# Windowed attention and a gated feed-forward on one core: another opening order, group 0's gate by Gelu, and four more blocks' x transposed by TensorE

## The chip, the core and the metric

The kernel runs on one core of a Trainium2 chip. The time is that of the device in microseconds for one execution, median of several. A profile of one execution gives each engine's instructions; the engines are TensorE (PE for matmuls, PEld for weight loads), VectorE (DVE), ScalarE (ACT), GpSimd (POOL) and SyncE (SP, which here only issues DMAs).

## The reference

Attention with 4 sink keys and a window of 128 keys, then a feed-forward layer with the quick Gelu. Inputs are float32; q, k and v are 4 x 8 x 768 x 64.

```python
scores = scale * np.matmul(q, k.transpose(0, 1, 3, 2))      # scale = 1/8
keep = is_sink | in_window                                    # key < 4, or 0 <= query - key < 128
scores = np.where(keep, scores, -1000000000.0)
a = np.exp(scores - np.max(scores, axis=-1, keepdims=True))
a = a / (np.sum(a, axis=-1, keepdims=True) + 1e-09)
x = np.matmul(a, v)        # heads side by side: 3072 x 512
h = x @ w_in               # 512 x 2048
g = h * (1.0 / (1.0 + np.exp(-1.702 * h)))
return g @ w_out           # 2048 x 512
```

## The kernel before

The 3072 rows are 24 blocks of 128 queries (6 for each of the 4 batch entries) and 12 groups of two blocks. All matmuls are in float16.

**Loads.** POOL issues, with a cast on the way, q, k and v of each block and the two weights in four pieces each (`w_in`, `w_out`). Block 0's q and k are loaded raw by SP (`rawq`, `rawk`) and cast by ACT or DVE. SP also issues the constants (`ident`, the mask `bias0`, `later`, and others), the DMA transposes and the outputs.

**Attention of a block.** q and k are transposed: for blocks 0 to 7 by PE (`tq`, L442, then a copy by ACT or DVE into `qkT`), for the rest by a DMA transpose. PE makes the scores of the 8 heads against the block's own keys (`own`, two tiles of 4 heads) and against those of the block before (`prv`), and against the sinks (`snk`). For block 0 PE first writes the mask into `own` (L489). DVE merges `own` and `prv` into one tile, since each query needs one of the two for each column (L565), takes the maximum (`mx`, L577), joins that of the sinks, and subtracts it (`e`, L632); ACT takes exp (`a`, L664). For blocks 0 to 3 one of the two halves is not subtracted by DVE: ACT takes exp from `own` with the maximum as bias, head by head (L618, bias `nb`). The result is transposed (`at`): by PE for blocks 0 to 3 (`ta`, L727), by DMA from SP for the rest (L761). POOL splits `at` into the columns of the own and of the previous block by two selects (L676 into `atp`, L670 in place). PE multiplies by v (`av`, L782 for the sinks, L788, L792), with a column of ones that gives the sum; DVE divides (L803, L804) into `xn`. `xn` is transposed into `xT`: by PE for blocks 0 to 3 (`tx`, L817, and a copy), by one DMA transpose for each group of two blocks after that (L830).

**Feed-forward of a group.** Eight units of `hT` (L852, into tiles of a ring named mm), each followed by its gate into `gT`: by ACT's Gelu (L882), or, in group 0, by ACT's tanh (L866) and a DVE step (L873), since tanh lies in the table that exp uses and Gelu in another (ACT_TABLE_LOAD). Then 16 matmuls for each block of the group (`o`, L903), a copy to `osb` and a store.

**Order.** Every step is an `Op` with an engine (or a choice of two), a cost, dependencies and buffers. `Plan.run` is a list scheduler: at each time it takes for each engine the ready step with the lowest key, and the order that it finds is written out as fixed instruction lists for all engines. The keys are a long list of numbers in the file, `KEYS`. Nothing is rescheduled on the chip: an engine, or a DMA queue, that waits for one step holds all that stand behind it.

Of the kernel before, what the change touches and what calls it, by code (L numbers as in the profile page):

```python
# [11 lines left out]
FP32 = mybir.dt.float32  # L12
# [7 lines left out]
P = 128  # L20
D = 64
# [9 lines left out]
    tx=(0, 1, 2, 3),  # L31
# [4 lines left out]
    tanh=(0,),  # L36
# [6 lines left out]
    sel2=(),  # L43
    steady=8,
# [10 lines left out]
512 736 367 602 310 550 170 2 181 458 338 312 41 456 211 67 413 484 39 69 10 35 90 100 306 46 134 13 203 194 247 206  # L55
29 390 176 216 256 251 370 426 301 489 604 578 150 778 128 562 881 72 614 513 42 504 253 755 644 539 48 533 276 782
679 567 55 559 296 805 710 594 61 587 320 827 740 624 68 617 345 844 766 658 78 648 379 857 793 690 92 681 407 867
813 720 107 712 436 878 152 236 882 900 27 94 466 541 425 476 862 561 460 553 112 798 137 350 264 400 218 221 668
488 153 811 230 771 608 315 470 175 32 47 508 330 186 243 26 743 24 858 44 171 49 396 257 119 51 823 195 872 77 611
60 87 641 172 145 224 897 63 120 600 629 767 54 835 191 104 369 303 378 291 233 547 166 14 22 56 138 187 234 792 328  # L60
419 454 592 657 57 713 28 189 523 86 122 260 212 638 8 480 429 366 299 467 725 279 4 322 106 437 406 635 787 358 814
34 125 747 342 742 158 165 239 374 207 548 748 609 53 178 442 705 870 149 45 443 527 38 329 397 140 483 110 242 441
244 463 190 709 240 353 776 777 200 884 516 12 507 91 139 84 105 6 219 544 473 352 490 435 210 403 74 141 272 281 3
534 869 582 98 143 123 156 384 274 494 293 30 215 445 115 468 135 797 155 368 616 59 924 840 292 646 228 915 324 5
919 524 469 847 214 676 151 677 245 62 398 269 96 749 275 249 496 530 580 519 918 667 517 238 621 491 340 325 505
317 669 88 250 300 331 627 923 551 495 860 227 706 167 707 259 71 430 288 108 773 294 262 520 556 606 545 922 698
543 255 653 514 372 348 535 343 699 102 268 326 355 660 926 354 252 448 220 738 184 280 83 311 121 318 283 546 584
639 571 925 730 570 278 687 540 399 383 560 376 731 113 287 349 388 692 928 607 542 880 263 763 197 764 302 97 486
337 142 820 344 305 574 613 672 599 927 754 598 298 716 568 431 410 588 404 756 133 309 385 417 722 930 640 569 888
284 790 213 791 327 109 509 365 159 838 377 332 603 643 701 632 929 781 631 323 745 595 461 438 618 433 783 154 336  # L70
411 447 750 932 446 319 526 270 812 226 351 126 395 177 405 356 634 678 733 665 931 804 664 347 770 625 487 471 649
464 806 168 362 439 478 774 934 702 630 896 333 832 248 833 386 144 564 427 188 864 434 389 666 708 760 695 933 826
694 381 795 659 510 497 682 493 828 185 394 472 499 800 936 734 663 901 357 850 261 851 414 162 590 459 204 875 465
418 697 739 786 727 935 843 724 408 817 691 537 521 714 515 845 198 424 498 525 821 282 387 566 905 450 492 273 82
908 877 193 314 911 295 1 440 20 209 633 36 619 671 626 572 402 522 148 573 265 101 552 174 662 452 118 232 428 799
75 809 229 834 11 339 235 50 477 93 304 726 500 161 721 647 444 9 173 475 579 593 160 765 80 116 899 815 759 183 892
127 202 65 132 179 231 290 920 363 474 601 409 258 655 518 382 768 703 313 596 674 199 412 686 31 16 40 853 124 70
217 673 0 117 364 416 201 359 785 23 371 577 375 81 415 719 916 79 19 95 7 784 266 622 485 735 675 696 66 52 391 549
531 129 131 819 222 420 511 873 729 267 903 451 822 597 15 271 650 807 285 654 506 761 704 728 76 58 421 576 557 146
147 837 237 449 538 883 753 286 906 481 839 628 17 289 683 829 307 688 536 788 737 752 89 64 453 605 585 163 164 852  # L80
254 479 565 889 780 308 910 502 854 661 18 316 715 846 334 717 563 808 762 779 103 73 482 637 615 180 182 863 277
501 591 893 803 335 912 529 865 693 21 341 744 859 360 746 589 830 789 802 114 85 503 670 645 192 196 874 297 528
623 898 825 361 913 555 876 723 25 373 769 868 392 772 620 848 810 824 136 99 532 700 680 205 208 885 321 554 656
902 842 393 914 583 886 751 33 401 794 879 422 796 651 861 831 841 157 111 558 732 711 223 225 890 346 581 689 904
856 423 917 612 891 775 37 432 816 887 455 818 685 871 849 855 169 130 586 757 741 241 246 894 380 610 718 907 866
457 921 642 895 801 43 462 836 909 684 758 652 636 575
# [154 lines left out]
def kernel(  # L241
# [32 lines left out]
    plan = Plan(RING)  # L274

# [22 lines left out]

    def hw(key, cost, fn, xfer, **kw):
        return plan.add(SP, key, cost, fn, xfer=xfer, post=1.3, **kw)  # L300

    o_ident = hw(-99, 0.4, lambda: nc.sync.dma_start(ident, ident_d.ap()), 0.1)
    o_bias0 = hw(-98, 0.4, lambda: nc.sync.dma_start(bias0, bias0_d.ap()), 0.1)
    o_later = hw(-97, 0.4, lambda: nc.sync.dma_start(later, later_d.ap()), 0.1)
    o_bias1 = hw(-96, 0.4, lambda: nc.sync.dma_start(bias1, bias1_d.ap()), 0.1)
    o_kept = hw(-94.5, 0.4, lambda: nc.sync.dma_start(kept, kept_d.ap()), 0.1)
    o_own = hw(-95, 0.4, lambda: nc.sync.dma_start(ownm, own_d.ap()), 0.1)
# [14 lines left out]
    def sw(key, cost, fn, xfer, **kw):  # L322
        return plan.add(POOL, key, cost, fn, xfer=xfer, post=2.6, **kw)
# [12 lines left out]

    def load_block(which, b, key, after=0.0):
        bb, r = divmod(b, 6)
        i = b % 2
        src = {"q": q, "k": k, "v": v}[which][bb, :, r * P : (r + 1) * P, :].rearrange("h s d -> s h d")  # L340
        if which == "v":
            return sw(key, 0.88, lambda: nc.gpsimd.dma_start(v65[:, b, :, 0:D], src), 1.0, deps=[z_1], after=after)  # L342
        w = "qk".index(which)
        buf = qkn[b // 2]
        if b in CFG["f32"]:
            raw = const.tile([P, H, D], FP32, name=f"raw{which}{b}")
            o_raw = hw(-120 + w, 0.4, lambda: nc.sync.dma_start(raw, src), 0.9)
            return plan.add(
                {DVE: 0.45, ACT: 0.6}, -95 + w, 0, lambda e: copy(e, buf()[:, i, w], raw), deps=[o_raw], take=[buf]
            )  # L350
        return sw(
            key, 0.88, lambda: nc.gpsimd.dma_start(buf()[:, i, w], src), 0.9,  # L352
            take=[buf], after=after,
        )
# [70 lines left out]
    o_qkt, o_ks, o_own_s, o_x = {}, {}, {}, {}  # L425

    for b in range(NBLK):
# [8 lines left out]
        if b in CFG["tq"]:  # L436
# [8 lines left out]
            for w in range(2):  # L445
                a = plan.add(
                    PE, K0 - 48 + w, 0.45 if b < 2 else 0.35, lambda w=w, f=t_qk: f(w), deps=[ld["qk"[w] + str(b)], o_ident],
# [37 lines left out]
        snk = ps("mi", (P, 4, 2, 4), FP32, f"snk{b}")  # L485
# [18 lines left out]
        if b in CFG["pemask"]:  # L504
            s_msk = plan.add(
                PE, K0 - 41, 0.9 if b == 0 else 0.43, lambda own=own, f=masks: f(own), deps=[o_bias0, o_identb] + (o_qkt[b] if b else []), take=own,
                slack=slack["s"],
            )
        s_own = None if both else plan.add(
            PE, K0 - 40, 0.5 if b < 2 else 0.24, lambda b=b, own=own, f=scores: f(own, b),  # L510
# [26 lines left out]
        if r > 0:  # L537

            def sinks(b=b, bb=bb, snk=snk):
                for j in range(4):  # L540
                    nc.tensor.matmul(snk()[:, j], qk_of(b)[:, j], ksb[:, bb, j], start=True, stop=True)

            s_snk = plan.add(PE, K0 - 40, 0.15, sinks, deps=([s_own] if b >= CFG['steady'] else []) + o_qkt[b] + [o_ks[bb]], take=[snk], give=[qkt[g]], slack=slack["s"])
# [69 lines left out]
        for l in range(2):  # L613
            if l >= 2 - nb:

                def exps(l=l, own=own, a16=a16, nbias=nbias):
                    for j in range(4):
# [7 lines left out]
                        ACT, K0 - 36.5, 1.02, exps, deps=[o_nb, z_a[b % RING["a16"]]],  # L625
# [18 lines left out]
        if r > 0:  # L644
# [9 lines left out]
            subs.append(plan.add(DVE, K0 - 38.7, 0.15, sub_s, deps=[top], take=[e32], give=[snk]))  # L654
# [99 lines left out]
        else:  # L754
            o_exp = plan.add(
                ACT, K0 - 36, 1.02, lambda a16=a16, e32=e32, w=w, f=exp: f(a16, e32, 0, w),
                deps=subs + zero, take=[a16], give=[e32], table="exp", slack=slack["e"],
            )
# [3 lines left out]
                deps=[o_exp], take=[at], give=[a16], xfer=1.35, post=0.8,  # L762
# [49 lines left out]
        if b in CFG["tx"]:  # L812
# [6 lines left out]
            o_tx = plan.add(PE, K0 - 28, 0.35, t_x, deps=norms, take=[tpx], give=[xn])  # L819
# [108 lines left out]
    order = plan.run()  # L928
    with tc.manual_schedule():
        for op in order:  # L930
            op.emit(op.on) if len(op.eng) > 1 else op.emit()
# [35 lines left out]
```

## Time and profile before

| what | value |
|---|---|
| median of 3 runs | 240.04 us (239.17 to 246.06) |
| the profiled execution | 240.28 us, its span 238.6 us |
| PE busy | 216.5 us (91%) |
| DVE busy | 141.2 us (59%) |
| ACT busy | 133.8 us (56%) |
| POOL busy | 114.2 us (48%) |
| mean granted TensorE clock | 0.985 |
| table loads on ACT | 20 of 1.28 us |

The span is cut into 40 slices of about 6 us; a digit is the busy share of an engine in one slice in tenths. The windows list for each stretch the stretch, its length, then busy time with the number of instructions for PE, PEld, DVE, ACT and POOL, the granted clock, the busy time of the DMA engines and the rate in GB/s. The chain gives start, length, and what the end of the program is traced back to.

### The profile page before, as it was taken

What the parts mean: (1) busy time and instruction counts of PE and PEld (TensorE: products, weight loads), DVE (VectorE), ACT (ScalarE), POOL (GpSimd) and SP (SyncE); (2) the same over time, 40 slices, a digit from 0 to 9 for tenths busy, and PEclk for the clock granted to TensorE, in tenths of its full rate; (3) what the DMA queues carried; (4) which work ended last, traced back from release to release, by engine and by line L of the source; (5) the groups of instructions that cost most, each with busy time, mean ns of one, the idle gap of its engine ahead of it and who ended that gap; (6) DMA issues with size and microseconds to landing.
All of it is one profiled execution on the core that took longest, in us unless ns stands there. A gap on an engine that the chain in (4) does not pass through costs nothing.

```text
span 238.6 us, 5359 instructions
## 1 busy us (share of the span) xinstructions
PE 216.5 (91%) x2173; PEld 152.6 (64%) x2173; DVE 141.2 (59%) x344; ACT 133.8 (56%) x203; POOL 114.2 (48%) x130
## 2 busy tenths in 40 slices
PE   0368899899977999999999999999999999999994
PEld 0237598777436758648659568578577685685763
DVE  4279989827934556788598639767676571120000
ACT  3256686577226665737837565565666648351521
POOL 8878689199505618619708449644051210700000
PEclk9999769999999999999999999999999999999999
DMA  8999999999999997999999999999992223530202
GB/s 115 182 161 192 199 200 179 138 127 115 133 157 256 149 152 140 149 195 161 140 171 171 163 204 178 143 180 173 124 206 47 49 64 69 145 91 0 88 3 88
DMA packets 134152, 33.38 MB, mean 140 GB/s; under 512 B 126672, under 2 KB 131184, under 8 KB 134128
## 3 DMA queue, kind: packets, MB, share of 16 engines
q0 software_dynamic: 77024, 13.37, 73.8%
q1 hardware_dynamic: 57104, 19.67, 46.0%
q8 instruction: 17, 0.28, 0.5%
q14 instruction: 7, 0.06, 0.1%
HBM read 27.49 MB, written 6.29 MB: 142 GB/s over the span
## 4 chain that ended last, share of the span: by engine, by line
PE 76%; DMA 10%; DVE 7%; ACT 3%; SPq 1%; issue 1%; ACTq 0%; DVEq 0%
PE hT L852 33%; PE o L903 29%; DMA xT<-xn 7%; DMA bias<-cbias 3%; PE av L788 2%; PE av L792 2%; PE av L782 2%; PE own L522 2%; DVE mx L577 2%; DVE own L565 1%; DVE gT L873 1%; PE prv L522 1%; DVE xn L804 1%; DVE e L632 1%; PE ta L727 1%; PE tq L442 1%
## 5 line engine op out<-in xcount | busy, mean ns | idle before, releaser
L852 PE MATMUL hT<-xT,w_in 128*128 128x256 f16 (+1 forms) x832 | 93.5, 265 | 2.6 <-DMA xT<-xn 2.2
L903 PE MATMUL o<-w_out,gT 128*128 128x512 f16 (+1 forms) x400 | 90.2, 371 | 0.0
L852 PEld LDWEIGHTS <-w_in 128*128 128x128 f16 x832 | 74.6, 98 | 15.9 <-DMA xT<-xn 3.2
L882 ACT ACTIVATE gT<-hT 128x512 f16<-128x512 f32 x88 | 51.8, 597 | 41.7 <-PE hT L852 41.6
L676 POOL TENSOR_SCALAR_AFFINE_SELECT atp<-at 128x1024 f16<-128x1024 f16 (+1 forms) x23 | 22.5, 979 | 89.0 <-DMA at<-a 76.8
L903 PEld LDWEIGHTS <-gT 128*128 128x128 f16 x400 | 36.9, 98 | 35.0
L565 DVE COPY_PREDICATED own<-later,prv 128x512 f32<-128x512 uint16 x40 | 26.0, 691 | 18.0 <-PE prv L522 17.2
L577 DVE TENSOR_REDUCE mx<-own 128x4 f32<-128x512 f32 x48 | 31.1, 683 | 2.0 <-PE own L497 1.9
L664 ACT ACTIVATE a<-e 128x1056 f16<-128x1056 f32 (+3 forms) x27 | 24.5, 918 | 13.8 <-DVE e L632 6.8
L632 DVE TENSOR_TENSOR e<-own,mx 128x512 f32<-128x512 f32 x44 | 28.7, 682 | 0.5
L329 DVE COPY osb<-o 128x512 f32<-128x512 f32 (+1 forms) x7 | 4.6, 654 | 32.6 <-PE o L903 30.3
L333 ACT COPY osb<-o 128x512 f32<-128x512 f32 (+1 forms) x16 | 9.1, 572 | 25.8 <-PE o L903 25.8
L670 POOL TENSOR_SCALAR_AFFINE_SELECT at<-at 128x1024 f16<-128x1024 f16 (+1 forms) x23 | 22.4, 972 | 1.6
L342 POOL DMA_DIRECT2D v<-in_v_dram x24 | 21.7, 913 | 0.0
L352 POOL DMA_DIRECT2D qkn<-in_q_dram x23 | 21.0, 911 | 1.1 <-POOLq L948 0.8
L804 DVE TENSOR_TENSOR xn<-av,rcp 128x256 f16<-128x256 f32 x48 | 20.4, 425 | 1.7
L352 POOL DMA_DIRECT2D qkn<-in_k_dram x23 | 20.6, 898 | 0.3 <-DMA qkn<-in_q_dram 0.2
L803 DVE RECIPROCAL rcp<-av 128x4 f32<-128x4 f32 x48 | 8.4, 176 | 18.0 <-PE av L792 17.2
L788 PE MATMUL av<-v,at 128*128 128x65 f16 x192 | 17.5, 198 | 0.1
L788 PEld LDWEIGHTS <-at 128*128 128x128 f16 x192 | 14.9, 100 | 1.3
L442 PE MATMUL tq<-ident,qkn 128*128 128x128 f16 x64 | 7.6, 282 | 8.8 <-DMA ident<-cident 8.8
L792 PE MATMUL av<-v,atp 128*128 128x65 f16 x160 | 15.4, 197 | 0.0
(57 smaller groups left out, 180.7 us busy)
## 6 DMA issues: line engine op xcount, KB each, us to landing
out_dram<-osb SPq DMA_DIRECT2D x23, 256.0 KB, 2.6
v<-in_v_dram POOLq DMA_DIRECT2D x24, 128.0 KB, 6.2
qkn<-in_q_dram POOLq DMA_DIRECT2D x23, 128.0 KB, 6.3
qkn<-in_k_dram POOLq DMA_DIRECT2D x23, 128.0 KB, 5.7
w_in<-in_moe_w_in_dram POOLq DMA_DIRECT2D x4, 512.0 KB, 8.6
w_out<-in_moe_w_out_dram POOLq DMA_DIRECT2D x4, 512.0 KB, 11.2
at<-a SPq DMA_TRANSPOSE x20, 3.5
rawk<-in_k_dram SPq DMA_DIRECT2D x1, 256.0 KB
```

The costliest lines, as they stand in the source:

```text
L352: key, 0.88, lambda: nc.gpsimd.dma_start(buf()[:, i, w], src), 0.9,
L565: nc.vector.copy_predicated(out=own[l](), mask=later.unsqueeze(1).to_broadcast((P, 4, P)), data=prv[l]())
L577: lambda l=l, own=own, small=small: nc.vector.tensor_reduce(out=small[:, l], in_=own[l](), axis=AX.X, op=ALU.max),
L632: nc.vector.tensor_tensor(out=e32()[:, 512 * l : 512 * l + 512].rearrange("p (j s) -> p j s", j=4), in0=own[l](), in1=small[:, l].unsqueez ...
L664: nc.scalar.activation(out=a16()[:, lo:hi], in_=e32()[:, lo:hi], func=AF.Exp, scale=scale)
L670: nc.gpsimd.affine_select(out=dst()[:, lo : lo + n], in_=at()[:, lo : lo + n], pattern=[[0, n], [1, P]], compare_op=ALU.is_ge, fill=0.0, b ...
L676: nc.gpsimd.affine_select(out=dst()[:, lo : lo + n], in_=at()[:, lo : lo + n], pattern=[[0, n], [-1, P]], compare_op=ALU.is_gt, fill=0.0, ...
L788: nc.tensor.matmul(av()[:, j], ato()[:, c], v65[:, b, h], start=(r == 0), stop=(r == 0))
L804: nc.vector.tensor_tensor(out=xn()[:, i].rearrange("p (j l) d -> p l j d", l=2)[:, l], in0=av()[:, :, 0:D], in1=rcp.unsqueeze(2).to_broadc ...
L852: nc.tensor.matmul(ht()[:, n], w_in16[:, c, bass.ts(f, P)], xt[g]()[:, tok, c], start=(c == 0), stop=(c == 3))
L882: lambda fs=fs, cols=cols, gt=gt, ht=ht: nc.scalar.activation(out=gt()[:, fs[0] : fs[-1] + 1, cols], in_=ht(), func=AF.Gelu_apprx_sigmoid),
L903: nc.tensor.matmul(po(), gt()[:, F, bass.ts(t, P)], w_out16[:, F, cols], start=(F == 0), stop=(F == NF - 1))
```

## The change

- Four blocks more (4 to 7) have x transposed by PE and copied, where groups 2 and 3 used the DMA transpose.
- Group 0's gate is ACT's Gelu; the DVE step and the tanh are gone.
- Raw q of block 0 is SP's first DMA, raw k the first on ACT's queue; `ident` and `bias0` follow on SP, and the table `kept` is not loaded.
- PE gets matmuls on a zeroed tile (`fill`) into columns 256 to 511 of a bank whose first 32 columns hold the sinks' scores. Their number ahead of each step comes from the gaps of PE in the plan between 1.5 and 45; there are 38, of which 15 are PE's first instructions.
- Some costs that the plan works with are changed, and `KEYS` is another list, so the order of all engines' work is another. In the first blocks, PE takes a unit of `hT` of group 0 before block 2's scores, and POOL issues the four pieces of `w_out` after block 1's selects.
- The division of the first blocks' shift between DVE and ACT (`nb`) is as before. `chain` is set so that it does nothing, and the cuts of exp in the last part of the diff are one piece wherever they are used.

```diff
 CFG = dict(
-    tx=(0, 1, 2, 3),
+    tx=(0, 1, 2, 3, 4, 5, 6, 7),
...
-    tanh=(0,),
+    tanh=(),
...
+    fill=(1.5, 45.0, 0.15, 0.11),
+    chain=99,
+    gap=3,
...
 KEYS = [ (another list of the same length and kind)
...
+    misc = psp.tile([P, 512], FP32, tag="mi", bufs=1, name="misc")
...
-    o_ident = hw(-99, 0.4, lambda: nc.sync.dma_start(ident, ident_d.ap()), 0.1)
...
+    raw, o_raw = {}, {}
+    for b in CFG["f32"]:
+        for w, e in (("q", nc.sync), ("k", nc.scalar)):
...
+            o_raw[w, b] = hw(-3000, 0.4, lambda dst=raw[w, b], src=src, e=e: e.dma_start(dst, src), 0.7)
+    o_ident = hw(-2000, 0.4, lambda: nc.sync.dma_start(ident, ident_d.ap()), 0.1)
+    o_bias0 = hw(-1999, 0.4, lambda: nc.sync.dma_start(bias0, bias0_d.ap()), 0.1)
...
+    fill = const.tile([P, 2 * P], FP16, name="fill")
+    z_f = plan.add(DVE, -2000, 0.1, lambda: nc.vector.memset(fill, 0.0))
...
-        snk = ps("mi", (P, 4, 2, 4), FP32, f"snk{b}")
+        snk = Buf("mi", lambda: misc[:, 0:32].rearrange("p (j l s) -> p j l s", l=2, s=4))
...
     order = plan.run()
+    idle, last = {}, 1.0
+    if CFG["fill"]:
+        lo, hi, rest, one = CFG["fill"]
+        for op in order:
+            if op.on == PE:
+                a, z = max(last, lo), min(op.start, hi)
+                for b in o_snk:
+                    if o_snk[b].start < z and o_sub[b].done + 0.5 > a:
+                        a = max(a, min(z, o_sub[b].done + 0.5))
+                idle[op] = max(0, int((z - a - rest) / (one if a > 6.0 else 2 * one)))
+                last = op.end
     with tc.manual_schedule():
         for op in order:
+            for n in range(idle.get(op, 0)):
+                nc.tensor.matmul(misc[:, 256:512], fill[:, 0:P], fill, start=True, stop=True)
             op.emit(op.on) if len(op.eng) > 1 else op.emit()
```

## The prediction, made before the changed kernel was run

> **What bounds the kernel now.** First the page's busy shares and the 40 slices (6 us each), to see which engine is full when.
>
> ```profile
> PE 216.5 (91%) x2173; PEld 152.6 (64%) x2173; DVE 141.2 (59%) x344; ACT 133.8 (56%) x203; POOL 114.2 (48%) x130
> ...
> PE   0368899899977999999999999999999999999994
> ...
> DVE  4279989827934556788598639767676571120000
> ...
> PEclk9999769999999999999999999999999999999999
> ```
>
> PE is full from slice 8 to the last one, except in slices 11 and 12; before slice 8 it is not, and there DVE is. So two stretches can give time: the start, and 66 to 75 us. From 90 us on PE has no idle time that the windows show, so nothing is won there unless PE has less to do. The profiled execution took 240.28 us with a span of 238.6; the median of the runs is 240.04, so I work from 240.28 and treat the two as equal.
>
> Next the chain of waits over the start, which says what opens it:
>
> ```profile
> 4.51 6.83 DMA bias<-cbias
> 11.38 1.01 PE own L489 x2
> 12.39 0.43 PE tq L442 x4
> 12.82 0.56 PE own L497 x8
> 13.40 1.30 DVE mx L577 x2
> ```
>
> The first maximum runs at 13.40 because the mask table, the last of eight transfers at the head of SP's queue, lands at 11.38. From there to 46.85 (the end of block 5's second subtraction) DVE is busy without a real gap: windows of 3 us show 2.66 to 2.97 from 15 to 45. That is the bound of the first stretch.
>
> Then the second stretch, as windows (PE busy first) and as the chain:
>
> ```profile
> 66.00:69.00 3.00, 2.50 (x12) 0.94 (x10) 0.90 (x2) 1.54 (x2) 0.00 (x0) 1.00 2.56 143
> 69.00:72.00 3.00, 1.59 (x20) 0.76 (x20) 1.49 (x3) 0.53 (x1) 0.00 (x0) 1.00 2.01 159
> 72.00:75.00 3.00, 1.75 (x16) 1.58 (x17) 0.99 (x2) 1.94 (x3) 0.83 (x1) 1.00 0.72 231
> ...
> 87.00:90.00 3.00, 2.64 (x32) 1.87 (x32) 0.14 (x1) 2.92 (x4) 1.18 (x2) 1.00 0.88 214
> ```
>
> ```profile
> 63.02 10.19 DMA xT<-xn
> ...
> 81.31 6.41 DMA xT<-xn
> 87.77 1.92 PE hT L852 x16
> ```
>
> PE loses 0.50, 1.41, 1.25 and 0.36 us, 3.5 in all, while x of groups 2 and 3 is on its way through the DMA transpose (10.2 and 6.4 us; the median over the run is 3.6).
>
> **The change, part by part.**
>
> *Constants and first loads.* K of block 0 moves from SP to ACT's queue, q to the head of SP's, ident and the mask behind it; the 64 KB table that nothing uses goes. Before, raw k alone at the head of SP's queue was cast 3.0 us after its issue (0.80, 3.82), raw q 5.7 us after (2.39, 8.07). Both now start near 0.8: landing between 3.8 and 6.5; I take 5.3, as they share the engines. Two casts of 0.62 end at 6.5, ident (before: 0.73 after raw q) near 6.0. Then transpose of q to 6.4, masks to 7.0, transpose of k to 7.4, its copy (0.59) and two fill groups to 8.2, scores 0.4, first maximum near 9.0 (bounds 7.6 and 11.0). Lead: 13.40 - 9.0 = 4.4 us. ACT's DMA issue (0.44) lies ahead of its table load (1.28), both done by 3.
>
> *Fill matmuls.* 38 of 128x256 into an unused half of the sinks' bank. Each is 0.11 us at the rate of hT (0.87 for 8) and 0.2 cold (masks: 0.5 for 512 columns). Fifteen (about 3.2 us) run before any data is there, hidden by the loads. The other 23 (2.5 us; 4.6 cold) stand in PE's order where it waits for ACT or DVE, seven of them ahead of block 1's previous-key scores and seven ahead of x's first transpose. Cover gone, they cost their 2.5. What they can buy: four transposes take 0.63 at 12.19, 0.40 at 25.49, 0.58 at 30.54 and 0.39 at 41.40, and the granted clock is 0.50 from 27 to 33. PE is not the bound there, so I count shorter steps only inside the chain above.
>
> *Gelu instead of tanh in group 0.* Eight DVE steps of 0.68 (L873) go. ACT's step is 0.60 either way (L866 and L882), but the exp and gate tables now alternate: counting in ACT's new order up to block 5's exp and the load after it, there are four more loads of 1.28, 5.1 us. ACT's work from the first maximum to that exp sums to 26 us by rows against some 33 of DVE, so I give the loads no cost; without that cover they cost 5.1.
>
> The Trainium skill, page "ScalarE: Activation LUTs", section "What ACT_TABLE_LOAD costs", speaks against this: it adds a drain of about 1.38 us to each switch. Here the exp of block 5 starts at 46.87 and lasts 1.08, the load runs at 47.97 for 1.28, the gate at 49.27: no drain shows. By the page ACT's sum would be 5.5 higher, 31.5, nearly DVE's; by the trace it stays at 26.
>
> *DVE's sum to the end of block 5's subtractions.* Before: 33.45 us for 38 wide steps, 3 copies, 8 normalizations, 20 small ones. After, in the new order: 32 wide (eight gates less; one output copy and the sink table of V, which POOL built, more), 10 copies, the rest alike. -6 x 0.64 + 7 x 0.42 + 0.2 = -0.7 us.
>
> *New order.* PE now takes group 0's first hT unit and seven fills before block 2's scores (before: hT at 32.6, block 2's merge on DVE at 19.70). Block 1's exp bias would be ready at 14.2 (before 19.29); exps 1.14, small and half exps 0.75, two copies 1.2, values and normalization 1.2 end at 18.5. DVE then waits for fills 0.8, transposes 0.4, copy 0.6, hT 0.9, scores 0.7: 3.4, less 0.6 of other steps: 2.8 idle. In exchange PE is ahead: when block 5's subtractions end it has passed some 10 more second matmuls of group 0 (2.2 us) and is two hT units of group 1 short (1.74): +0.5. On POOL, three q/k loads (0.9 each) now stand between the two select pairs of block 1, and w_out behind them; by issue and landing (6.2 and 11.2 us medians) they come at or just before their use, cost 0, bound 3.
>
> Stage one: 4.4 + 0.7 - 2.8 + 0.5 = 2.8 us.
>
> *x of blocks 4 to 7 by PE.* Two DMA transposes go, so SP's queue has two fewer entries ahead of the score transposes (at) and the outputs. Sixteen matmuls come: 0.22 for four in the chain, 0.9 us. Four copies (0.42 on DVE or 0.58 on ACT) fall in a stretch where DVE is busy 0.9 to 1.5 of 3. The 3.5 us of idle go if the next late thing, at of blocks 6 and 7, is in time: PE has both halves of group 1's output to do meanwhile. Gain 3.5 - 0.9 = 2.6.
>
> From 90 us on: the same instructions, the same kind of tail (16 half-width matmuls, a copy, a DMA): 0.
>
> Sum: 2.8 + 2.6 = 5.4; 240.28 - 5.4 = **234.9 us**, 2.1% below the median. About 2% (4.8 us, to 235.2) is also what a measurement of this kernel can tell from no change.
>
> **The rivals.**
>
> *DVE does not wait in the start.* For it: the loads and scores of block 2 could come by the time block 0 is normalized, and a warm PE shortens the steps that I counted. Against it: PE's order is fixed, hT first. The 2.8 come back: 232.1.
>
> *The head start is lost.* Seven loads of 128 KB and two of 512 KB go out on POOL while the raw blocks land; if these take as long as raw q did and the constants as long as the mask did (6.8 from issue), the lead is near 1.6 instead of 4.4: 237.7. Against it: fewer bytes stand ahead in SP's queue.
>
> *ACT becomes the bound.* Blocks 2 and 3's exps stand behind four gates of group 0 on ACT, between two loads. If all four added loads lie on the path: 234.9 + 5.1 = 240.0. Against it: 26 of 33 us. By the Trainium skill's figure, with the drain on all four, it would be 245.5.
>
> *w_out comes late: slower than before.* One mechanism: the four w_out loads, issued before at 18.66, 20.14, 25.53 and 32.62, now stand on POOL behind both select pairs of block 1 and three q/k loads that each wait for a queue place. PE meets group 0's first second-stage matmul near 35, and it stands ahead of block 2's transposes and block 5's scores. With 3 us of wait at each of the three loads (half a median landing), the first w_out is issued at 34.3, lands 11.2 later at 45.5, and PE and all behind it is 10.3 late: 245.2. It makes the kernel slower from a landing 5.4 past 35.2. For it: POOL already waited 1.7 us for a place at w_in. Against it: that was the only such wait over 1 us.
>
> *x by PE does not do what it says:* if at of blocks 6 and 7 sets the end of that idle, 3.5 stays and 0.9 is paid: 238.4.
>
> **How the numbers follow.** Forecast 0.45, of which 0.36 beyond the 2% mark; no DVE wait 0.20; lost head start 0.07; ACT 0.06; x by PE in vain 0.05; late w_out 0.17, nearly all beyond 2% on the slow side. Faster 0.36 + 0.20 = 0.56; slower 0.17; within 2% the rest, 0.27. The range runs from 230.7 (no DVE wait and the early bound, 232.1 - 1.4) to 241.5 (ACT's case with 1.5 of fills uncovered); the forecast's own is 231 to 238.
>
> **What would show it.** First maximum near 9 us (a start past 11 ends the first step); fills in PE's row and 0.4 for four transposes throughout; no xT DMA before group 4 and PE busy 3 of 3 from 66 to 75; a DVE gap of some 3 us ahead of block 2's merge; four more table loads before 50 us, each 1.28 with nothing behind. The forecast is wrong if PE waits on w_out or on ACT's gates before 50 us, if hT of group 2 starts later than 70 us, or if PE idles after 90.

## The result, and the profile after

The changed kernel takes 238.75 us (median of 20 executions, 237.68 to 240.54) against 240.97 us for the kernel before in the same session (20 executions): a ratio of 0.9917, with an interval of 0.9895 to 0.9938. It is faster, by 0.8% where 2.1% was forecast, and so inside the 2% that the forecast called hard to tell from no change. The ratio leaves out the few executions in a slower state, so it is not quite that of the medians. The profiled execution takes 237.68 us with a span of 236.0: 2.6 us off the span instead of 5.4.

The page of the changed kernel, as shares and slices of 5.9 us:

```profile
PE 220.2 (93%) x2227; PEld 154.7 (66%) x2227; DVE 138.5 (59%) x346; ACT 137.1 (58%) x203; POOL 113.0 (48%) x129
...
PE   5939769999799999999999999999999999999994
...
DVE  5481898958548868857479189865657462130000
...
PEclk9767999999999999999999999999999999999999
```

Two things differ from before. DVE, which was 7 to 9 tenths busy in every slice from 12 to 48 us, now has a slice of 1 tenth at 18 to 24 us. And PE's hole at slices 11 and 12 is gone, but a smaller one stands at slice 10. The windows (PE, PEld, DVE, ACT, POOL, granted clock, DMA share, GB/s) show both, and a half clock at 15 to 21 us:

```profile
12.00:15.00 3.00, 0.00 (x0) 0.00 (x0) 2.90 (x9) 0.76 (x2) 1.28 (x2) 0.86 1.38 196
15.00:18.00 3.00, 2.48 (x21) 1.99 (x22) 1.98 (x6) 2.69 (x8) 0.88 (x1) 0.50 2.10 171
18.00:21.00 3.00, 3.00 (x25) 2.50 (x24) 0.61 (x2) 1.03 (x4) 1.64 (x3) 0.51 1.59 196
...
57.00:60.00 3.00, 1.71 (x12) 0.90 (x10) 2.27 (x4) 0.66 (x2) 2.07 (x2) 1.00 0.91 212
60.00:63.00 3.00, 2.37 (x39) 1.62 (x40) 1.29 (x5) 0.00 (x0) 2.93 (x4) 1.00 0.61 115
66.00:69.00 3.00, 3.00 (x20) 1.56 (x19) 0.95 (x4) 2.99 (x3) 1.54 (x2) 1.00 2.18 139
69.00:72.00 3.00, 3.00 (x36) 2.08 (x35) 1.31 (x2) 2.53 (x4) 0.00 (x0) 1.00 1.65 170
```

So from 66 to 75 us PE does what the forecast said: 3 of 3. The 1.92 us of idle at 57 to 63 were not in it. The chain of waits over the start of the changed kernel, from the first scores to block 2's merge on DVE (L588, L565 before):

```profile
8.22 0.54 PE own L520 x8
...
18.81 1.49 PE misc L971 x7
20.30 0.44 PE tx L845 x4
...
20.77 0.59 ACT xT L348
...
21.40 1.05 PE hT L880 x16
22.46 0.33 PE own L520 x8
22.79 0.24 PE prv L520 x8
...
23.12 0.69 DVE own L588
```

The first maximum runs at 8.80 (13.40 before), 4.6 us ahead. Block 2's merge runs at 23.12 (19.70 before), 3.4 us behind. Ahead of it stand seven fills, x's transpose and its copy, and one hT unit.

For DVE, from the first maximum to the end of block 5's last subtraction:

| kernel | stretch, us | length | DVE busy | DVE idle |
|---|---|---|---|---|
| before | 13.40 to 46.85 | 33.45 | 31.81 | 1.64 |
| changed | 8.80 to 47.85 | 39.05 | 30.34 | 8.71 |
| before, with the new start only | 10.42 to 42.70 | 32.28 | 31.18 | 1.10 |
| changed, block 2's scores moved ahead | 8.45 to 45.05 | 36.60 | 30.41 | 6.19 |

DVE has 1.5 us less to do, and 7.1 us more of waiting. Its waits of 8 to 48 us in the changed kernel (total, times, longest):

```profile
DVE own L588 <- PE prv L520: 4.4, 2, 3.6
...
DVE own L588 <- PE own L520: 1.3, 2, 0.7
DVE rcp L831 <- PE av L816: 1.2, 1, 1.2
DVE at L344 <- PE ta L751: 0.7, 1, 0.7
DVE qkT L344 <- PE tq L465: 0.5, 1, 0.5
```

The longest of these, 3.6 us, is the wait that the forecast had counted, as 2.8; it had none of the others.

### The profile page after: what moved, and what is told of

Same layout as the page of the kernel before. It is cut to its first block, busy times and chain, and to the rows that moved or that the text cites. A ratio compares the mean times of both kernels' runs of the same rounds, so it can differ in the third digit from the quotient of the medians.

```text
span 236.0 us, 5468 instructions
## 1 busy us (share of the span) xinstructions
PE 220.2 (93%) x2227; PEld 154.7 (66%) x2227; DVE 138.5 (59%) x346; ACT 137.1 (58%) x203; POOL 113.0 (48%) x129
## 4 chain that ended last, share of the span: by engine, by line
PE 76%; DVE 8%; POOL 7%; issue 5%; DMA 2%; ACT 1%; SPq 0%; DVEq 0%; POOLq 0%; ACTq 0%
PE o L931 32%; PE hT L880 29%; DVE own L588 2%; PE av L816 2%; POOL at L694 2%; PE own L545 2%; POOL atp L700 2%; DMA ident<-cident 2%; PE misc L971 2%; POOL qkn L375 2%; DVE mx L600 2%; PE av L820 2%; PE av L810 2%; PE prv L545 1%; POOL v L366 1%
## 5 line engine op out<-in xcount | busy, mean ns | idle before, releaser
L880 PE MATMUL hT<-xT,w_in 128*128 128x256 f16 (+1 forms) x832 | 94.5, 264 | 0.2 <-ACT xT L348 0.2
L910 ACT ACTIVATE gT<-hT 128x512 f16<-128x512 f32 x96 | 56.9, 597 | 53.9 <-PE hT L880 53.5
L880 PEld LDWEIGHTS <-w_in 128*128 128x128 f16 x832 | 73.4, 98 | 13.0 <-issue 0.5
L588 DVE COPY_PREDICATED own<-later,prv 128x512 f32<-128x512 uint16 x40 | 26.0, 692 | 31.7 <-PE prv L545 25.2
L688 ACT ACTIVATE a<-e 128x1056 f16<-128x1056 f32 (+3 forms) x27 | 24.0, 920 | 1.4 <-DVE e L655 0.5
L348 ACT COPY osb<-o 128x512 f32<-128x512 f32 (+1 forms) x19 | 10.7, 564 | 23.1 <-PE o L931 16.0
L820 PE MATMUL av<-v,atp 128*128 128x65 f16 x160 | 14.9, 193 | 0.0
```

The source lines that it names most:

```text
L588: nc.vector.copy_predicated(out=own[l](), mask=later.unsqueeze(1).to_broadcast((P, 4, P)), data=prv[l]())
L688: nc.scalar.activation(out=a16()[:, lo:hi], in_=e32()[:, lo:hi], func=AF.Exp, scale=scale)
L880: nc.tensor.matmul(ht()[:, n], w_in16[:, c, bass.ts(f, P)], xt[g]()[:, tok, c], start=(c == 0), stop=(c == 3))
L910: lambda fs=fs, cols=cols, gt=gt, ht=ht: nc.scalar.activation(out=gt()[:, fs[0] : fs[-1] + 1, cols], in_=ht(), func=AF.Gelu_apprx_sigmoid),
```

## The experiments

Every ratio is to the kernel before, with runs of both on the same chip; 0.01 is 2.4 us. The first four ask what in the changed kernel spends the lead of 4.6 us, the next four take parts alone, the last eight move what the first eight pointed at. In the edits, `TAG` gives a step of the plan a name: `TAG['tx', 0]` is x's transpose of block 0.

### Fills: none, and only the first 15

```diff
-            for n in range(idle.get(op, 0)):
+            for n in range(0):
```

> The changed kernel without any fill matmul, all else in the same order. Theory 1 (fills cost: 3.9 us of them lie in the chain of waits between 8 and 23 us, and the clock is 0.5 from 15 to 21 us in spite of them): block 2's merge on DVE starts 1.5 to 3 us earlier than 23.1, and the whole is 1 to 2 us shorter than the changed kernel (about 237). Theory 2 (fills pay, since they keep PE at full clock elsewhere): the steps before 12 us run at half rate, the first maximum comes at 9.8 or later instead of 8.8, the half clock lasts longer than 15 to 21, and the whole is 1 us or more longer (240). In both the stretch from 51 to 63 keeps its idle PE.

Measured: 0.9950 (0.9924 to 0.9976), span 236.8. Block 2's merge is at 23.25, no earlier: without fills the first hT unit runs at half clock and takes 1.86 us instead of 1.05. It starts 1.1 us earlier (20.30), but the half clock lasts to nearly 24 us here, and hT and the scores behind it take as much longer. So the seven fills stand on the chain, and without them as much is lost at half clock. In this order the fills are worth 0.3% or nothing, and they are not what spends the lead.

```diff
+    first_pe = next(op for op in order if op.on == PE)
...
-            for n in range(idle.get(op, 0)):
+            for n in range(idle.get(op, 0) if op is first_pe else 0):
```

> The changed kernel with only the fifteen fills ahead of PE's first transpose. Theory 1: as without fills, or up to 0.5 us better, since the first scores keep four transposes at 0.38 us: 236.5 to 237.5. Theory 2: the later fills are what pays, so 239.5 or more.

Measured: 0.9950 (0.9918 to 0.9983), span 237.2. Merge at 23.25 again, and a second stretch of half clock at 30 to 36 us.

### Thirty more fills where PE is idle from 12 to 15.5 us

```diff
+    idle[TAG['ta', 0, 0]] = 30
```

> The changed kernel with 30 more fills ahead of block 0's first transpose of exp, where PE stood idle from 11.9 to 15.5 us. If the half clock from 15 to 21 us comes from that idle time, four transposes stay at 0.4 us there, the ten fills of that stretch take 1.1 us instead of 2.5, and block 2's merge starts 1.5 to 2.5 us earlier than 23.1: total 236.5 to 237.5. If the clock is not what delays this stretch: 238.75 within 0.5.

Measured: 1.0030 (0.9998 to 1.0062), span 239.8. The fills did not fill the gap. They write the bank whose first columns hold the sinks' scores, and waited 3.85 us for DVE to have read these; then they ran at half clock for 5.1 us. The first hT unit came 2.15 us later, block 2's merge at 25.27, and the whole kernel 2.7 us later by ratio. What is added to PE's sequence ahead of block 2's scores arrives at the end here. Not all of it needs to come that way: block 5's merge is 3.6 us later (44.16), and the clock was at half again from 33 to 39 us.

### x of blocks 4 to 7 by DMA again, the rest as changed

```diff
+            if b in (4, 5, 6, 7):
+                o_tx.emit = lambda: None
...
+                        nc.sync.dma_start_transpose(
+                            xt[g]().rearrange("p i c t -> p (i c) t"), xn().rearrange("p i h d -> p (i h d)")
+                        )
```

> The changed kernel with x of blocks 4 to 7 again by one DMA transpose for each two blocks; the 16 PE transposes and 4 copies are left out, the order is otherwise the same. Theory 1 (the DMA transpose was the wait, and PE's transposes take it away): hT of group 2 starts 3 to 8 us later than 64.3, PE is idle there, total 2 to 4 us longer (241 to 243). Theory 2 (the wait has only moved to exp's transposes and selects, x by PE in vain): within 1 us of the changed kernel.

Measured: 1.0049 (1.0019 to 1.0080). Two readings. x by PE is worth 1.0049 - 0.9917, some 3.2 us (the intervals are 0.5 and 0.7 us wide on either side), so in this order the forecast's 2.6 was not too high. And the rest of the change (new start, order, Gelu, fills) is slower than the kernel before by 1.2 us, where the forecast had it 2.8 faster. Its windows show 3.45 us of PE idle at 66 to 72 and 84 to 90, as before the change, and 1.76 at 57 to 63 besides.

This run says one thing more. The edit touches nothing in the start, yet block 2's merge ran at 21.31, 1.8 us earlier than in the profile of the changed kernel, and block 5's at 40.59, no earlier (40.52 there): the granted clock was 0.72, 0.50 and 0.64 in the three windows from 27 to 36 us, where the changed kernel has 1.00. So an earlier merge is no gain by itself, and profiles of one order differ by more than a microsecond here.

### The parts alone, in the order of the kernel before

The new start:

```diff
-            o_raw = hw(-120 + w, 0.4, lambda: nc.sync.dma_start(raw, src), 0.9)
+            o_raw = hw(-120 + w, 0.4, lambda: (nc.scalar if w else nc.sync).dma_start(raw, src), 0.9)
...
+    first = [TAG['raw', 0], TAG['raw', 1], o_ident, o_bias0, o_later, o_bias1, o_own]
+    order = first + [op for op in order if op not in first and op is not o_kept]
```

> The kernel before, with raw k on ACT's queue, raw q at the head of SP's, ident and the mask behind it and the unused table left out; order and everything else as before. First maximum near 9 us instead of 13.4. Theory 1 (a lead at the start is spent on PE and DVE waits before 50 us whatever the order is, since loads and the chain through PE set the pace): 0.993 to 1.000 (0 to 1.7 us). Rival (the new order and the Gelu of group 0 spend it, and with before's order DVE, which is full from 15 to 45 us, passes the lead on): 0.982 to 0.988 (2.9 to 4.4 us).

Measured: 0.9901 (0.9860 to 0.9941), between the two theories. The first maximum is at 10.42, 3.0 us earlier, and the lead grows to 4.1 us at group 1's first hT (46.08 before, 41.96 here). DVE waits 1.1 us in all over the stretch of the table. So before's order, with its tanh, passes the lead on in full up to there; 2.4 us of it reach the end. A part is lost at 81 to 87 us, where PE idles 1.55 us for the DMA transpose of group 3's x; the kernel before idled 0.36 at 87 to 90.

x of blocks 4 to 7 by PE:

```diff
...
+            tpx = psp.tile([P, 4, P], FP16, tag="pv", bufs=RING["pv"], name=f"tx{2 * g + i}")
+            for c in range(4):
+                nc.tensor.transpose(tpx[:, c], xn()[:, i].rearrange("p h d -> p (h d)")[:, bass.ts(c, P)], ident)
+            nc.vector.tensor_copy(out=xt[g]()[:, i], in_=tpx)
```

> The kernel before, with x of blocks 4 to 7 transposed by PE (four transposes of a block into the ring of values, a copy by DVE) in place of the DMA transpose; nothing else changes. Theory 1 (this part alone earns more than the whole change, and the rest of the change loses): PE's idle in 66-75 and 87-90 us, 3.5 us, goes and 0.9 is paid: ratio 0.986 to 0.990 (237.0 to 238.0 us). Rival (it earns so much only together with the new start and order): 0.993 to 1.000.

Measured: 0.9921 (0.9888 to 0.9954), a little less than expected. Of the 3.5 us of idle in the kernel before, 1.35 had ended with another DMA transpose, that of q and k of group 4, and only 1.82 and 0.36 with x's:

```profile
69.85 0.23 PE L522 MATMUL own<-qkT 64*128 64x128 f16 x2 [1.35 <-DMA qkT<-qkn]
...
73.25 2.79 PE L852 MATMUL hT<-xT,w_in 128*128 128x256 f16 x24 [1.82 <-DMA xT<-xn]
```

With x by PE the two waits for x are gone and the other stands, now 1.83 us (its transfer is 10.98 us long in the chain, from 58.78):

```profile
69.81 0.23 PE L534 MATMUL own<-qkT 64*128 64x128 f16 x2 [1.83 <-DMA qkT<-qkn]
```

Both:

> The kernel before, with both parts that earned alone: the new start (0.9901) and x of blocks 4 to 7 by PE (0.9921); tanh in group 0, no fills, before's order. Theory 1 (the start's lead passes on in before's order, and the idle that x by PE removes is there for it too): the two multiply, 0.980 to 0.985 (236 to 237.2 us against 240.9), better than the changed kernel's 0.9917. Rival (both are spent on the same idle of 66-90 us): no better than the larger one, 0.987 to 0.992.

Measured: 0.9848 (0.9783 to 0.9912). They add up, with no new order, no fills and no Gelu. By ratio this is at least level with the changed kernel; the intervals overlap.

Both, with Gelu in group 0 in place of tanh:

```diff
-                        out=th(), in_=ht().rearrange("p f t -> p (f t)"), func=AF.Tanh, scale=0.851
+                        out=gt()[:, fs[0] : fs[-1] + 1, cols], in_=ht(), func=AF.Gelu_apprx_sigmoid
...
-                    lambda fs=fs, cols=cols, gt=gt, ht=ht, th=th: nc.vector.scalar_tensor_tensor(
+                    lambda: None,
```

> As the run with the new start and x by PE, and group 0's gate by Gelu on ACT in place of tanh and a DVE step, at the place of the tanh in before's order. Eight DVE steps (5.4 us) go, and table loads of 1.28 come between exps and gates. Theory 1 (what the changed kernel loses lies in its order, not in the Gelu): within 1 us of the run without it, 0.978 to 0.986. Rival (the loads that switch ACT between exp and Gelu are the loss): over 1 us slower than the run without it, 0.987 to 1.000.

Measured: 0.9899 (0.9849 to 0.9949), 1.2 us over the run without it, with intervals that overlap. The traces point the same way: from 20 to 50 us PE waits 2.7 us for ACT's gates, where it waited 0.2 without Gelu, and at 51 us it has 2.2 us more of work left. So Gelu gains nothing in that order and probably costs. This run has the changed kernel's start, x by PE and Gelu, and before's order without fills: against 0.9917 no difference is shown.

### Tanh in the changed kernel, and block 4's exp earlier

```diff
-                        out=gt()[:, fs[0] : fs[-1] + 1, cols], in_=ht(), func=AF.Gelu_apprx_sigmoid
...
+        nc.scalar.activation(out=th, in_=ht().rearrange("p f t -> p (f t)"), func=AF.Tanh, scale=0.851)
+        nc.vector.scalar_tensor_tensor(
```

> The changed kernel, with group 0's gate by tanh on ACT and a DVE step again, in the same order; all but one of the table loads ahead of 49 us go (5.1 us of ACT), eight DVE steps of 0.68 come back (5.4 us). Theory 1 (block 4's exp is late because it stands behind group 0's gates and a table load on ACT): the exp runs about 1.3 us or more earlier, the idle of PE at 57-63 (1.9 us) shrinks by as much, and against the kernel before 0.985 to 0.992. Rival (DVE is what paces 15 to 48 us in the new order too): DVE's 5.4 us fill its 8.7 us of idle at best in part, 0.992 to 1.003.

Measured: 1.0103 (1.0058 to 1.0148). Both theories failed. Block 5's merge goes back from 40.52 to 45.39. From 20 to 50 us DVE waits 5.0 us for ACT's tanh ahead of the gate's DVE steps, and PE 1.8 us for these steps and 2.9 for `xn`, which stands on DVE with them; the clock is below full from 27 to 39 us besides. So taking out most of the table loads gained nothing; the Gelu is worth 4.5 us in this order.

```diff
+    place = max([TAG['gate', 0, 5]] + TAG['exp', 4][0].deps, key=order.index)
+    move(TAG['exp', 4][0], place)
+    move(TAG['dat', 4], TAG['exp', 4][0])
```

> As the run with the tanh gate, and block 4's exp with its DMA transpose moved up on ACT and SP, right behind the gate of unit 5 of group 0, instead of behind all eight. Theory 1: the transpose of block 4's scores is issued before 44 us instead of 47.0, lands by 54 instead of 57.9, and PE's idle at 57-63 (1.9 us) is under 0.5; 1 to 2 us less than without the move. Rival (the transposes land late since POOL's eight loads of 42 to 49 us share the DMA engines): issued earlier, it lands no earlier than 56, and the idle stays over 1 us.

Measured: 1.0129 (1.0085 to 1.0174). Block 4's select came at 53.42 and PE did not idle at 57 to 63, but it had not done so in the run above either, whose start is too late for it. The pair tells nothing on the late `at`; the next edits do.

### Block 2's scores ahead of group 0's first hT

```diff
+    put(TAG['tq', 2, 1], TAG['tx', 0])
+    put(o_qkt[2][1], TAG['tx', 0])
+    behind = order[order.index(TAG['tx', 0]) + 1]
+    put(TAG['own', 2], behind)
+    put(TAG['prv', 2], behind)
+    idle[TAG['tx', 0]] = 4
```

> The changed kernel, with block 2's second group of q/k transposes and its copy moved ahead of x's first transpose, and block 2's two score steps right behind that transpose, ahead of group 0's first hT (1 us), three fills fewer. Theory 1 (DVE paces 23 to 48 us, so its wait of 3.6 us ahead of block 2's merge sets the later steps): the merge comes near 21.5 instead of 23.12 and the end of block 5's subtraction 1 to 1.6 us earlier, ratio 0.984 to 0.989. Rival (what comes later is set by other waits, as where x went by DMA: merge at 21.3, block 5's no earlier): 0.990 to 0.995.

Measured: 0.9829 (0.9776 to 0.9881), 236.34 us, better than expected and 2.1 us under the changed kernel by ratio. DVE's row of the merge, in the changed kernel and then here:

```profile
23.12 0.69 DVE L588 COPY_PREDICATED own<-later,prv 128x512 f32<-128x512 uint16 x1 [3.63 <-PE prv L520]
```

```profile
19.59 0.70 DVE L589 COPY_PREDICATED own<-later,prv 128x512 f32<-128x512 uint16 x1 [1.22 <-PE prv L521]
```

The wait falls from 3.63 to 1.22, and block 5's merge from 40.52 to 37.72. Part of this is not the edit: the first maximum was 0.35 us earlier here, and the clock was full again at 18 us instead of 21. The time of the whole rests on six executions, with an interval that lies just below the changed kernel's.

The same with x of blocks 4 to 7 by DMA, stage one alone:

> The changed kernel with block 2's scores moved ahead, and x of blocks 4 to 7 by the DMA transpose: stage one alone, mended. The same without the scores moved gave 1.0049. Theory 1 (stage one's miss is block 2's scores standing behind hT): 0.993 to 0.998, 1.5 to 2.5 us less than 1.0049. Rival (the gain of the moved scores comes only with x by PE): 1.002 to 1.006.

Measured: 1.0021 (0.9985 to 1.0058) against 1.0049 without the move: 0.7 us, inside both intervals. Here the move gains nothing that can be told, as the rival said: PE waits 5.4 us for these DMA transposes, the longest time 3.26.

### The loads beside block 4's DMA transpose

In the changed kernel block 4's exp stands on ACT behind the last of group 0's gates and a table load, though its input is complete at 39.85. ACT's rows, and POOL's first select of block 4:

```profile
43.98 0.60 ACT L910 ACTIVATE gT<-hT 128x512 f16<-128x512 f32 x1 [1.87 <-PE hT L880]
44.59 1.28 ACT L688 ACT_TABLE_LOAD   x1
45.89 1.08 ACT L688 ACTIVATE a<-e 128x1056 f16<-128x1056 f32 x1
```

```profile
57.86 1.09 POOL L700 TENSOR_SCALAR_AFFINE_SELECT atp<-at 128x1024 f16<-128x1024 f16 x1 [8.96 <-DMA at<-a]
```

The DMA transpose is issued at 47.00 and the select starts 10.86 us later; POOL issues eight loads of 128 KB from 41.9 to 48.9. Four of these, V of blocks 6 to 9, moved behind block 4's select:

```diff
+    vs = [ld["v" + str(n)] for n in (6, 7, 8, 9)]
+    order = [op for op in order if op not in vs]
+    at = order.index(TAG['sel', 4]) + 1
+    order[at:at] = vs
```

> The changed kernel, with the four loads of V for blocks 6 to 9 (half of the bytes that POOL issues from 42 to 49 us) moved behind block 4's select. Theory 1 (at of block 4 is late because its exp runs late on ACT; other loads stretch the DMA transpose only in part): it still lands after 56 us and PE's idle at 57-63 (1.9 us) stays over 1 us: 0.988 to 0.993. Rival (the loads on the DMA engines make it take 10 us): it lands by 54.5, the idle is under 0.5, 0.981 to 0.986.

Measured: 0.9865 (0.9823 to 0.9908). The select starts at 52.98, as the rival said, but the idle stays at 1.29: the four loads now take 3.5 us of POOL between block 4's selects and block 5's. Behind both pairs (`TAG['sel', 5]`):

> The changed kernel, with the four loads of V for blocks 6 to 9 behind the selects of blocks 4 and 5 (behind block 4's alone, block 5's select waited 3.5 us for their issue). Theory 1 (PE's idle of 1.9 us at 57-63 is the late at of block 4, whose DMA transpose shares the engines with these loads): both selects are done before 57, PE's idle there is under 0.3, 0.982 to 0.986 (1.3 to 2 us less than the changed kernel). Rival (what stands behind the idle is set elsewhere, and the next wait takes it): 0.988 to 0.992.

Measured: 0.9838 (0.9791 to 0.9885), 236.57 us, span 234.3. The transpose is issued at 46.32 and lands within 6.5 us, and PE has no idle at 57 to 63:

```profile
52.83 1.09 POOL L701 TENSOR_SCALAR_AFFINE_SELECT atp<-at 128x1024 f16<-128x1024 f16 x1 [7.85 <-DMA at<-a]
```

The select starts 5.0 us earlier than in the changed kernel, with the exp in the same place of ACT's order. In this run 0.87 us of idle come instead at 69 to 72, for `at` of the next group.

### Both, with and without fills

> The changed kernel with both edits: block 2's scores ahead of group 0's first hT, and the four V loads behind both selects. Theory 1 (two separate losses, one ahead of 48 us and one at 54-60): they add up, 0.973 to 0.978 (234.2 to 235.4 us against 240.7), PE without idle from 33 to 87 us. Rival (they are one: with the scores earlier, at of block 4 is on time by itself): 0.981 to 0.985.

Measured: 0.9806 (0.9775 to 0.9837), 236.10 us: the fastest here, its interval below the changed kernel's, but not below those of the two single edits. They did not add up to the 0.973 to 0.978 expected. Each edit did its part: the merge waits 1.86 us instead of 3.63, and the idle at 54 to 60 us, 2.17 with the scores moved alone, is 0.38. But in the profiled execution the first maximum was at 9.42, the half clock lasted from 15 to 21 us again, and x of a later group comes late at 168:

```profile
168.30 1.05 PE L881 MATMUL hT<-xT,w_in 128*128 128x256 f16 x8 [1.18 <-DMA xT<-xn]
```

Whether the moved loads cause this last wait is not shown: the run without fills, with the loads in their old place, has 1.36 us of it.

> As the run with both edits, without any fill matmul. Theory 1 (fills keep the granted clock up at 6 to 12 us but buy little, since DVE paces what follows): within 0.4% of the run with both. Rival (with the scores moved, PE's steps of 15 to 21 us are on DVE's path, and half clock there costs): 0.5 to 1% slower.

Measured: 0.9921 (0.9882 to 0.9960), 2.8 us more than with fills, so here the fills are worth more than the 0.3% of the first run, and more than the rival gave them. Block 5's merge is 0.6 later (40.27 against 39.65), as half clock in 15 to 24 us would do. The larger part is elsewhere: at 168 to 171 PE idles 2.17 us for x by DMA instead of 1.18, and the granted clock of the next 3 us is 0.50. Whether that follows from the fills or only from other timing, these two profiles don't tell.

## Why the forecast was too good

**Stage one, forecast 2.8 us: 1.9.** PE is the bound again from 36 us on, so its work left at 51 us tells how far ahead the changed kernel is: 180.6 us of busy time are left before, 179.6 after, of which 0.9 are the sixteen transposes of x that the kernel before does not have. So it is 1.9 us ahead. These are two single profiles, and the other runs with the same start give 1.7 to 2.7.

- The lead at the first maximum was right: 9.0 forecast, 8.80 measured, and 8.45 to 9.61 in the other runs with this opening.
- The step that failed is the new order's price on DVE. The forecast put one wait there, 2.8 us ahead of block 2's merge, ending at 21.9. That wait measures 3.63 and ends at 23.12, and there are six more of 0.5 to 1.2 us each: over the stretch DVE's idle is up by 7.1, not 2.8. The sum of DVE's work was if anything cautious (-0.7 forecast, -1.5 measured). So block 5 ends at 47.85, 1.0 later than before, instead of 2.3 earlier.
- That stage one lost only 0.9 of its 2.8 is luck: a second term was wrong the other way. The forecast gave PE's exchange +0.5. When block 5's subtractions end, PE has some 2.7 us less of work left than before at that point; by 51 us it has done some 30 second matmuls of group 0, where the kernel before had done 16.
- How far the cause is shown. In every profile of the changed order with Gelu, DVE's idle in this stretch is 6.2 to 12.5 us; the stretch is 36.6 us long or more, against 32.9 with the same start, x and Gelu in before's order, where block 5 ends at 43.45 (DVE idles 6.0 us there, as the gate's eight steps are gone). So the order makes DVE late. That hT and fills ahead of block 2's scores are a part of it is shown from both sides: 30 fills more there cost 2.7 us at the end, the scores ahead of hT give 2.1 back. But that move takes DVE's idle only from 8.71 to 6.19; what the other waits come from no run takes apart. With the loads moved too, or with x by DMA, the move's gain is inside the intervals. And at the end the two orders with Gelu, 0.9917 and 0.9899, can't be told apart.
- What was overlooked besides is that PE's own waits there bring half clock: from 12 to 15.49 it waits 3.57 us for DVE, and the fills, costed at 0.11 each, run at 1.49 for seven.

**Stage two, forecast 2.6 us: 0.7.** This is the larger miss. The idle at 66 to 75 and 87 to 90 us, 3.5 us, went; 0.38 came at 90 to 93, for a subtraction on DVE. The step that failed is "the 3.5 us of idle go if the next late thing, at of blocks 6 and 7, is in time". It was `at` of block 4, some ten microseconds ahead of the idle that went, and it took 1.92 back. From 51 to 93 us PE's idle falls from 3.54 to 2.31; the sixteen transposes cost 0.9, and the tail is 0.3 shorter: 0.7.

The forecast's reading of the 3.5 us was wrong in part too: 1.35 of it ended with the DMA transpose of q and k of group 4, not with x's. In the changed order PE takes these scores later (71.43 for 69.85) and does not wait for them; with x by PE alone the wait stayed.

Two things make block 4's `at` late. Its transpose shares the DMA engines with eight loads: with four of them out of the way the select starts 5.0 us earlier and the idle goes, so this is shown. Its exp runs at 45.89 (37.50 before), held on ACT by group 0's gates and a table load; what that alone costs is not shown, as the run that moved it started too late to tell.

**The sum.** 1.9 + 0.7 = 2.6, the difference of the spans. The run with x by DMA is not stage one alone: at 51 us it is 1.7 us ahead, and it loses that to 1.7 us more of idle than before up to 93 us and 1.0 behind.

**The rivals.** "No DVE wait" went the wrong way. "The head start is lost" has the right size (237.7 for the profiled 237.68) by luck, with the wrong mechanism: the loads were in time, and the start lost its lead later. "ACT becomes the bound" was partly there: its sum did not matter, but one exp stood late behind gates and a load, a queue effect that a sum of 26 against 33 us can't show. One of the forecast's own signs of being wrong also showed, though small: at 31 us PE waits 0.69 us for a gate of ACT. w_out was not late: no wait of PE names it. The four added loads cost 1.28 each and no drain: one runs from 21.88 to 23.16 between a copy that ends at 21.87 and a gate that starts at 23.18. By the Trainium skill, page "ScalarE: Activation LUTs", section "What ACT_TABLE_LOAD costs", some 1.38 us more would lie there; this trace again shows none.

**Gelu, costed at nothing on ACT.** In the changed order it is more than free: without it the kernel is 4.5 us slower. In before's order it wins nothing, and PE waits 2.7 us for ACT's gates. What a part is worth depends on the order that it stands in.

## What to carry to other kernels

A lead at the start is worth what the order behind it lets through: list every wait of the engine that paces the stage, in the new order, and not only the one at the place that was edited. When a stall is removed, look for the next late thing in order of time, and for what moves it: look at its place in its engine's queue and at the transfers issued beside it. Where a change has several parts, cost them together with their order; here the new start and x by PE, put into the old order, did at least as well as all of it, and two small moves in the new order won another 0.8 or 0.9% each, though not both at once.

## What the runs showed of the hardware

- The granted clock fell to 0.50 for 15 to 21 us after PE had waited 3.57 us, in spite of 23 fills around it. The Trainium skill, page "TensorE: Matmul & The Clock Gate", section "Part 1: The HAM clock gate", gives half rate after an idle window of about 3.4 us, and this agrees. The same wait gave 0.82 and 0.61 in another profile, whose order is the same up to there, and 0.57 came once after a wait of 2.40 behind a window with 0.60 us of work. In the kernel before the clock fell to 0.50 at 27 us, with no wait of PE over 0.8 us since 18.
- The DMA transpose of block 4's exp took 10.86 us from issue to its first reader beside eight loads of 128 KB (9.35 to 11.0 in six other profiles), and 5.6 to 6.5 beside four, in three profiles.
- Kernels with the same opening had their first maximum between 8.45 and 9.61 us. With the same order and fills block 2's merge ran at 21.31 to 23.12. A milestone that moves by a microsecond or two between two single profiles is no evidence of an edit.
